# Reads of the turned exponentials and query loads from a second queue, early blocks turned in half steps 4, 5 and 12

## The chip, the cores and the metric

The kernel runs on one core of one Trainium2 chip. The metric is the device time of one execution in microseconds (us), as the median of repeated runs. Before the change it is 977.36 us (three runs, 975.66 to 977.53).

## What is computed

Packed attention followed by a Fourier mixing step and a feed-forward network, all in float32. `B` is 8, `S` is 576, there are 8 heads of 64 and 32 packed queries; `dm` is 512.

```
packed = softmax(p k^T / 8) v            # 32 rows for each head
x      = softmax(q packed^T / 8) packed  # 576 rows for each head
u      = x + real(fft(fft(x, axis=1), axis=2))
un     = (u - mean(u)) / sqrt(var(u) + 1e-6)
out    = u + relu(un @ w_ch1) @ w_ch2    # 512 -> 2048 -> 512
```

## The kernel before

The rows of all eight batches are cut into blocks of 128: four for each batch (`E0`, `O0`, `E1`, `O1`) and one `R` for each pair of batches, 36 in all. Four blocks make a tile of the feed-forward network, so there are nine tiles, t = 0 to 8. Tile 0 is batch 0. From tile 2 on a tile straddles batches: tile 6, for example, is E1 and O1 of batch 5, the R of batches 4 and 5, and E0 of batch 6.

`ffn` runs one tile. For each of 16 column chunks j it does `up(j)` (twelve matmuls into the single PSUM bank `ph`, L903), then `down(j - 1)` (twelve matmuls into four banks `acc`, L920). Every float32 product is three float32r products of a high and a low part. After `up(j)`, ScalarE makes `hh` (L909) and VectorE makes `hl` (L910); both read `ph`, so `up(j + 1)` may begin only when `hl` is done. The high and low parts of the weights (`wr_h` by ScalarE at L107, `wr_l` by GpSimd at L110) are made again for every tile, three pairs ahead.

Between the parts lie 32 half steps: `step(2j)` stands between `up(j)` and `down(j - 1)`, `step(2j + 1)` behind `down(j - 1)`. During tile t each half step advances the generator `front(t + 1)`, the attention and the transforms of the next batch, by one piece; half steps 1 and 2 finish the batch before it (its R block). The string `ORDER` lists the pieces, and each `y` is the end of one half step. For the batches from 2 on, which are made in tiles 1 to 6, half step 0 holds the scores and exponentials of two groups of four heads (`S`) and their way through memory (`D`); half step 3 holds `X`; 4 holds `p0 p1`, the matmuls of `packed` (`po`, L417); 5 the transposes `pptp` (`d0 d1`); 6 the first products `pg` (`g0`); 7 the score matmuls of the queries (`U`, tiles `s2T` and `s2Tt`); 12 to 15 `m0 a0 m1 a1`.

`D` is `scores_away`. The exponentials must stand with the keys on the partitions. VectorE transposes them in 32x32 pieces (`e1b`, L370), SyncE writes each group to memory (`fare`, L374, one DMA for each group), and four DMAs for each group read them back in turned order (`e1T`, L381). The first `po` matmuls read the `e1T` of group 0, the next ones that of group 1. All these DMAs, and the two query loads `qt` behind them, are on SyncE's queue in this order.

The blocks of the next tile, too, must be turned before the tile begins. `Turned.send(i)` does it for block i: VectorE subtracts the mean (`unp`, L827), transposes 32x32 pieces (`unt`, L830), SyncE writes them away (`far`, L832) and reads them back in four DMAs (`back`, L837). `sends(i)` calls `send_next` as often as half step i occurs in `SENDS`, and `send_next` takes the first block that isn't sent and whose mean is known; if there is none, nothing is sent. At the beginning of tile t those blocks of tile t + 1 are known that belong to earlier batches: one in tiles 1 and 2, two in tiles 3 and 4, three in tiles 5 and 6, all four in tile 7.

The order on TensorE, VectorE, ScalarE and GpSimd is the order in which the code is written. On SyncE a scheduler sets it, save for DMAs that are pinned with `keep_in_program_order`. `bd`, `unp`, `turned` and other tiles share one tag (`tmp`) of three buffers; `qt` and the keys `kp` share one (`ld`) of two; `e1`, `e1b`, `e1T` share one (`att`) of four.

Of the kernel before, what the change touches and what calls it, by code (L numbers as in the profile page):

```python
# [9 lines left out]
F32 = mybir.dt.float32  # L10
# [7 lines left out]
P = 128  # L18
S = 576
HS = S // 2  # L20
D = 64
NPK = 32
DM = 512
ATT = 4
# [17 lines left out]
         "H1 v2 W10 P1",  # L42
         "K0 K1 Q0 Q1 y S V0 V1 y X y p0 p1 y d0 d1 y g0 y U y g1 y e0 y e1 y y m0 y a0 y m1 y a1 y f0 y r0 y h0 y f1 y r1 y "
         "h1 y y",
         "V0 V1 S D Q0 Q1 y X y p0 p1 y d0 d1 y g0 y U y g1 y e0 y e1 y y m0 y a0 y m1 y a1 y f0 y r0 y h0 y f1 y r1 y "
         "h1 y y")


# [3 lines left out]
TOPS = [1, 1, 1, 1, 2, 1, 1, 2, 1, 1, 0, 1, 1, 1, 1, 1, 0, 1, 0, 1, 0, 1, 1, 0, 1, 1, 0, 0, 0, 0, 0, 0]  # L52
BITS = [2, 2, 1, 3, 1, 2, 1, 1, 1, 0, 1, 2, 1, 1, 0, 1, 0, 1, 0, 0, 0, 1, 2, 2, 0, 1, 1, 0, 0, 0, 0, 0]
SQUARES = [4, 7, 12, 16]
SENDS = (5, 12, 15, 27, 27)
NJ = 16
MANUAL = {getattr(mybir.EngineType, n) for n in ("PE", "DVE", "Activation", "Pool")}
NE = 288
# [25 lines left out]
def tile_kernel(ctx, tc, kpT, qT, v, w1, w2, tabH, tabL, tabR, tabF, tabB, tabT, sel, ident_d, out):  # L84
    nc = tc.nc
    B = kpT.shape[0]
# [4 lines left out]
    work = ctx.enter_context(tc.tile_pool(name="work", bufs=2))  # L91
# [59 lines left out]
    def spot(n, part, shape):  # L151

        t = (w1f, w2f, ubuf[:, 5:, :])[n].rearrange("p j n -> p (j n)")[:, int(part * DM):]
        size = shape[1] * shape[2]
        return t[:, 0:size].rearrange("p (a n) -> p a n", a=shape[1])
# [56 lines left out]
    def load_weights(i):  # L212

        for _ in range(BITS[i]):
            bits(*topped.pop(0))
            fetch_free()
        for _ in range(TOPS[i]):
            tops(*coming.pop(0))
# [10 lines left out]
    now = {}  # L229
# [10 lines left out]
    def next_step():  # L240
        steps[0] = (steps[0] or 0) + 1
        for item in [x for x in due if x[0] <= steps[0]]:
            due.remove(item)
            item[1]()
# [19 lines left out]
            after(1, squares)  # L264
            after(2, deviation)

    def load(src, shape, name, place=None, pinned=False):
        if isinstance(place, tuple):
            t = spot(*place, shape)
        elif place:  # L270
            t = work.tile(shape, F32, tag=place, name=name, bufs=2)
        else:
            t = ld.tile(shape, F32, tag="ld", name=name)
        sent = nc.sync.dma_start(t, src)
        if pinned:
            tc.keep_in_program_order(sent)
        return t
# [4 lines left out]
        nc.tensor.matmul(o, ll, rh, start=False, stop=last)  # L282

    def front(b):
        kps, vts, qts, e1s, e1T, rinv = {}, {}, {}, {}, {}, {}
        pp2s, ppT, pph, ppl, bdh, bdl = {}, {}, {}, {}, {}, {}
        s2s, zs, as_, fh, fl, xh, xl, oh, ol, gh, gl = {}, {}, {}, {}, {}, {}, {}, {}, {}, {}, {}
        eos, fs, sums = {}, {}, {}
# [11 lines left out]
        def load_keys(g):  # L300
            kps[g] = load(kpT[b, :, 2 * g:2 * g + 2, :], [P, 2, S + NPK], "kp")

        def load_values(g):
            if b < 2:
                vt = load(v[b, :, g], [P, 5, 4 * D], "vt", (g, 4) if b == 0 else None, b == 1)
                vts[g] = [vt[:, c] for c in range(5)]
                return
            vt = load(v[b, :, g, 0:4], [P, 4, 4 * D], "vt", "wst", True)
            vts[g] = [vt[:, c] for c in range(4)]
            vts[g].append(load(v[b, :, g, 4], [P, 4 * D], "vt4", ("xh", "oh")[g], True))  # L310

        def load_queries(g):
            qts[g] = load(qT[b, :, 2 * g:2 * g + 2, :], [P, 2, S], "qt", (g, 7) if b == 0 else (2, 0) if b == 1 and g == 0 else (2, 2 * S / DM) if b == 1 else None, b > 1)

        def side(g, h):

# [48 lines left out]
        def scores_away(*gs):  # L365

            blocks = {}
            for g in gs:
                blocks[g] = work.tile([P, S], F32, tag="att", name="e1b", bufs=ATT)
                nc.vector.transpose(blocks[g], e1s[g])  # L370
            fars = {}
            for g in gs:
                fars[g] = dr.tile([P, S], F32, tag="fare", name="fare")
                tc.keep_in_program_order(nc.sync.dma_start(fars[g], blocks[g]))  # L374
            for g in gs:
                e1T[g] = work.tile([P, 4, 5, NPK], F32, tag="att", name="e1T", bufs=ATT)
                wide = e1T[g].rearrange("k h c p -> k h (c p)")
                for r in range(4):
                    n = NPK * (5 if r < 3 else 3)
                    at = 5 * NPK * r  # L380
                    back = nc.sync.dma_start(wide[r * 32:(r + 1) * 32, :, 0:n],  # L381
                                             fars[g][:, at:at + n].rearrange("(h k) n -> k h n", h=4))
                    tc.keep_in_program_order(back)

        def turned_scores(*gs):
# [73 lines left out]
        def queries(*gs):  # L459

            for g in gs:
                if g not in qts:
                    load_queries(g)

            tails = [bank("s2Tt")] + ([psf.tile([P, 512], F32, tag="ph", name="s2Tt")] if len(gs) == 2 else [])
            s2T = narrow(gs, lambda g, h: ppT[g][side(g, h):side(g, h) + D, h * NPK:(h + 1) * NPK],
                         lambda g, h, w: qts[g][side(g, h):side(g, h) + D, h // 2, w], "s2T", dict(zip(gs, tails)))
            for g in gs:
                s2s[g] = work.tile([P, 18, 32], F32, tag="att", name="s2", bufs=ATT)
            for c, w in ((1, slice(16, 18)), (0, slice(0, 16))):  # L470
                for g in reversed(gs):
                    nc.vector.transpose(s2s[g][:, w, :].rearrange("p a k -> p (a k)"), s2T[g][c])  # L472
# [118 lines left out]
        def folded_parts(g):  # L591
# [10 lines left out]
            def low():  # L602
# [3 lines left out]
            in_place("H", g, low)  # L606

        parts = {"S": lambda _: scores(0, 1), "U": lambda _: queries(0, 1), "D": lambda _: scores_away(0, 1),
                 "s": scores, "t": turned_scores, "p": packed, "d": packed_parts, "q": queries, "e": less_one, "m": less_mean, "g": values_spectrum, "a": weights, "f": folded, "r": folded_rest,
                 "h": folded_parts,  # L610
                 "T": load_tables, "B": lambda _: load_turn(), "K": load_keys, "V": load_values,
                 "Q": load_queries, "I": lambda _: nc.sync.dma_start(ident, ident_d),
                 "W": lambda i: fetch(i // 2, i % 2), "w": lambda i: tops(i // 2, i % 2),
                 "v": lambda i: (bits(i // 2, i % 2), topped.remove((i // 2, i % 2))),
# [119 lines left out]
        for t, base in enumerate((0, FO) if b else ()):  # L734
# [15 lines left out]
            h = work.tile([P, DM], F32R, tag="tmp", name="yr_h", bufs=3)  # L750
# [120 lines left out]
    def wsplits():  # L871

        for t, _ in enumerate(tiles):
            for n, j in [(0, 0)] + [x for j in range(1, NJ) for x in ((0, j), (1, j - 1))] + [(1, NJ - 1)]:
# [4 lines left out]
                yield  # L879

    def ffn(first, turned, step, nxt, alone):
        keys = turned.keys
        n = len(keys)
# [46 lines left out]
        def sends(i):  # L930
            for _ in range(SENDS.count(i) if nxt is not None and first else 0):
                nxt.send_next()
# [45 lines left out]

    ready, splits = [], wsplits()
    gen0 = front(0)  # L980
    cur = Turned(tiles[0][1])

# [22 lines left out]
    with tc.manual_schedule(engines=MANUAL):  # L1005
        for at in gen0:
            if at == "means":
                less_blocks(0, 1)
                for i in (0, 1):
                    for move in cur.moves(i):  # L1010
                        move()
            elif at == "rest":
                break
        cur.parts(0)
        cur.parts(1)
        less_blocks(2, 3)
        next(splits)
        gens = {1: front(1)}
        next(gens[1])
    spare.clear()  # L1020
    rest = gen0
    for t, (first, tk) in enumerate(tiles):

        gen = gens.pop(t + 1, None) or (front(t + 1) if t + 1 < B else iter(()))
        ended = []

        def step(i):

            next_step()
            if i in ((1, 2) if t else (0, 2)):  # L1030
                next(rest, None)
            elif not ended and next(gen, None) == "rest":
                ended.append(gen)
            if t == 0:
                load_weights(i)
            assert i < 2 * NJ - 1 or t + 1 >= B or ended

        nxt = Turned(tiles[t + 1][1]) if t + 1 < len(tiles) else None

        with tc.manual_schedule(engines=MANUAL):  # L1040
            ffn(first, cur, step, nxt, t + 1 >= B)
        cur, rest = nxt, gen
# [114 lines left out]
```

## Time and profile before

| | |
|---|---|
| median of three runs | 977.36 us (975.66 to 977.53) |
| profiled execution | 979.0 us, of which the traced span is 977.2 us |
| granted TensorE clock | 0.993 on average |
| TensorE, VectorE, ScalarE, GpSimd busy | 950.1, 586.4, 453.0, 461.7 us |
| tiles 2 to 6 by the trace | 104 to 106 us each |

The trace is of one execution. A timeline row gives start and duration in us, engine (PE is TensorE, DVE VectorE, ACT ScalarE, POOL GpSimd, SPq SyncE's queue), line, operation, tiles written and read, and in brackets the idle time ahead of it with what ended it. Matmuls are pipelined: a 128x512 matmul is shown 0.39 us long, but the next one starts 0.227 us after it, so the last 0.16 us of a row are its tail.

### The profile page before, as it was taken

Reading aid. Unit: us, or ns where it says so; the run is one execution under the profiler, and the core shown is the slowest. Engines: PE = TensorE matmul, PEld = TensorE weight load, DVE = VectorE, ACT = ScalarE, POOL = GpSimd, SP = SyncE. Lnnn points to the kernel's source line nnn. Section 1 sums busy time; section 2 is a strip of 40 time slices with the busy share of each in tenths; the row PEclk is TensorE's granted clock in tenths of the full one; section 3 lists DMA queues with packets and bytes.
Section 4 is the critical chain, followed back from the end, with each engine's and each line's share of the span. In section 5 each row is a group of like instructions: output and inputs, shape, how many; then the busy total and the mean of one; then the engine's idle time right before and its main releaser. Section 6 shows DMA issues by size and latency. Waiting matters only on the chain.

```text
span 977.2 us, 15222 instructions
## 1 busy us (share of the span) xinstructions
PE 950.1 (97%) x5622; PEld 776.4 (79%) x5622; DVE 586.4 (60%) x1184; ACT 453.0 (46%) x930; POOL 461.7 (47%) x397
## 2 busy tenths in 40 slices
PE   7999999999999999999999999999999999999997
PEld 4777787788877887788778887878777888887886
DVE  5888966587567856594658566774569452223111
ACT  5677754445444445444534444444444443333231
POOL 3136534554455534653455445543464354544442
PEclk9999999999999999999999999999999999999999
DMA  9565312400152015200540035100601010101001
GB/s 356 213 223 189 104 65 77 142 29 1 47 192 73 1 43 166 103 22 2 165 146 22 1 101 163 70 22 23 195 22 44 11 55 22 44 23 44 1 1 43
DMA packets 47338, 79.70 MB, mean 82 GB/s; under 512 B 6928, under 2 KB 27280, under 8 KB 47264
## 3 DMA queue, kind: packets, MB, share of 16 engines
q1 hardware_dynamic: 46224, 77.42, 23.9%
q0 software_dynamic: 1040, 1.31, 0.4%
q8 instruction: 44, 0.72, 0.3%
q14 instruction: 30, 0.25, 0.1%
HBM read 58.92 MB, written 19.79 MB: 81 GB/s over the span
## 4 chain that ended last, share of the span: by engine, by line
PE 83%; DVE 9%; ACT 3%; DMA 2%; issue 1%; SPq 1%; POOL 0%; DVEq 0%; ACTq 0%
PE acc L920 35%; PE ph L903 35%; DVE hl L910 1%; DVE w2f L203 1%; PE px L282 1%; PE px L280 1%; PE px L281 1%; DMA wst<-w 1%; DMA e1T<-fare 1%; PE idle L723 1%; DMA ident<-ident_d 1%; PE py L280 1%; PE py L282 1%; PE py L281 1%; PE s2T L328 1%
## 5 line engine op out<-in xcount | busy, mean ns | idle before, releaser
L110 POOL TENSOR_TENSOR wr_l<-w2f,wr_h 128x512 fp32r<-128x512 f32 x144 | 188.8, 1311 | 296.3 <-ACT wr_h L107 296.0
L110 POOL TENSOR_TENSOR wr_l<-w1f,wr_h 128x512 fp32r<-128x512 f32 x144 | 198.7, 1380 | 187.7 <-ACT wr_h L107 163.0
L910 DVE SCALAR_TENSOR_TENSOR hl<-ph,hh 128x512 fp32r<-128x512 f32 x144 | 99.0, 687 | 293.4 <-ACT hh L909 292.2
L903 PE MATMUL ph<-uh,wr_h 128*128 128x512 f32 (+1 forms) x580 | 227.3, 394 | 6.5 <-DVE hl L910 3.9
L920 PE MATMUL acc<-wr_h,hh 128*128 128x512 f32 x576 | 226.0, 392 | 0.0
L903 PE MATMUL ph<-ul,wr_h 128*128 128x512 f32 (+1 forms) x580 | 224.6, 389 | 0.5 <-DVE ul L110 0.5
L903 PE MATMUL ph<-uh,wr_l 128*128 128x512 f32 (+1 forms) x580 | 224.9, 390 | 0.0
L920 PE MATMUL acc<-wr_h,hl 128*128 128x512 f32 x576 | 224.8, 390 | 0.0
L920 PE MATMUL acc<-wr_l,hh 128*128 128x512 f32 x576 | 224.8, 390 | 0.0
L909 ACT ACTIVATE hh<-ph 128x512 fp32r<-128x512 f32 x144 | 86.1, 598 | 244.6 <-PE ph L903 235.2
L107 ACT CAST wr_h<-w1f 128x512 fp32r<-128x512 f32 x144 | 89.3, 620 | 173.6 <-PE acc L920 86.3
L903 PEld LDWEIGHTS ph<-uh,wr_h 128*128 128x128 f32 x580 | 108.9, 189 | 36.5 <-DVE s L472 7.6
L903 PEld LDWEIGHTS ph<-uh,wr_l 128*128 128x128 f32 x580 | 108.9, 189 | 22.9
L920 PEld LDWEIGHTS acc<-wr_h,hl 128*128 128x128 f32 x576 | 108.1, 188 | 23.2
L903 PEld LDWEIGHTS ph<-ul,wr_h 128*128 128x128 f32 x580 | 108.6, 188 | 21.7 <-DVE ul L110 1.0
L920 PEld LDWEIGHTS acc<-wr_h,hh 128*128 128x128 f32 x576 | 108.1, 188 | 21.8
L920 PEld LDWEIGHTS acc<-wr_l,hh 128*128 128x128 f32 x576 | 108.2, 188 | 21.0
L107 ACT CAST wr_h<-w2f 128x512 fp32r<-128x512 f32 x144 | 88.3, 614 | 33.8 <-PE acc L920 26.6
L254 ACT ACTIVATE junk<-ubuf,stat 128x512 f32<-128x512 f32 x36 | 25.8, 718 | 4.5 <-DVE stat L249 4.5
L968 DVE SCALAR_TENSOR_TENSOR ubuf<-acc,stat,ubuf 128x512 f32<-128x512 f32 x36 | 24.6, 744 | 3.6 <-PE acc L920 3.5
L110 DVE TENSOR_TENSOR yl<-py,yh 128x258 fp32r<-128x258 f32 x32 | 13.1, 425 | 19.5 <-ACT yh L107 18.8
L827 DVE TENSOR_SCALAR unp<-ubuf,stat 128x512 f32<-128x512 f32 x26 | 24.2, 932 | 0.4
(230 smaller groups left out, 1220.7 us busy)
## 6 DMA issues: line engine op xcount, KB each, us to landing
kp<-kpT SPq DMA_DIRECT2D x16, 608.0 KB, 4.9
out<-ubuf SPq DMA_DIRECT2D x36, 256.0 KB, 4.0
qt<-qT SPq DMA_DIRECT2D x12, 576.0 KB, 4.4
far<-unt SPq DMA_DIRECT2D x26, 256.0 KB, 2.0
back<-far SPq DMA_DIRECT2D x104, 64.0 KB, 2.0
vt<-v SPq DMA_DIRECT2D x12, 512.0 KB, 3.9
w1f<-w SPq DMA_DIRECT2D x9, 512.0 KB, 6.2
w2f<-w SPq DMA_DIRECT2D x9, 512.0 KB, 5.7
```

The lines of the kernel that those rows point to most:

```text
L107: copied = nc.scalar.copy(hi, src)
L110: (lo_eng or nc.vector).tensor_tensor(lo, src, hi.bitcast(F32), ALU.subtract)
L254: nc.scalar.activation(junk, u, AF.Square, bias=st[:, 1:2], scale=-sign, accum_out=st[:, 2:3])
L280: nc.tensor.matmul(o, lh, rh, start=first, stop=False)
L281: nc.tensor.matmul(o, lh, rl, start=False, stop=False)
L282: nc.tensor.matmul(o, ll, rh, start=False, stop=last)
L827: nc.vector.tensor_scalar(un, u_of[key].rearrange("p (c q d) -> p q c d", c=4, q=4), stat_of[key][:, 1:2], None, ALU.subtract)
L903: nc.tensor.matmul(ph[:, t], l[:, c * P:(c + 1) * P], r[:, c, t], start=(k == 0), stop=(k == 11))
L909: nc.scalar.activation(hh[:, :T], ph[:, :T], AF.Relu)
L910: nc.vector.scalar_tensor_tensor(hl[:, :T], ph[:, :T], 0.0, hh[:, :T].bitcast(F32), ALU.max, ALU.subtract)
L920: nc.tensor.matmul(acc[i], l[:, w], r, start=(j == 0 and k == 0), stop=(j == NJ - 1 and k == 2))
L968: nc.vector.scalar_tensor_tensor(u, acc[i], stat_of[keys[i]][:, 2:3], u, ALU.mult, ALU.add)
```

## The change

The reads of group 1's exponentials leave `scores_away` and become a function `scores_back`, which half step 2 calls with ScalarE's queue; group 0's stay on SyncE in half step 0. The query loads go from half step 0 to half step 3 and to ScalarE's queue. `SENDS` becomes (4, 5, 12, 27, 27). This holds for tiles 1 to 6 (the batches from 2 on); `SENDS` acts in tiles 1 to 7.

```
-         "V0 V1 S D Q0 Q1 y X y p0 p1 y d0 d1 y g0 y U y g1 ...
+         "V0 V1 S D y X Q0 Q1 y p0 p1 y d0 d1 y g0 y U y g1 ...
...
-SENDS = (5, 12, 15, 27, 27)
+SENDS = (4, 5, 12, 27, 27)
...
-            qts[g] = load(qT[b, :, 2 * g:2 * g + 2, :], [P, 2, S], "qt", ..., b > 1)
+            qts[g] = load(qT[b, :, 2 * g:2 * g + 2, :], [P, 2, S], "qt", ...,
+                          queue=nc.scalar if b > 1 else nc.sync)
...
-            for g in gs:
-                e1T[g] = work.tile([P, 4, 5, NPK], F32, tag="att", name="e1T", bufs=ATT)
-                wide = e1T[g].rearrange("k h c p -> k h (c p)")
-                for r in range(4):
-                    n = NPK * (5 if r < 3 else 3)
-                    at = 5 * NPK * r
-                    back = nc.sync.dma_start(wide[r * 32:(r + 1) * 32, :, 0:n],
-                                             fars[g][:, at:at + n].rearrange("(h k) n -> k h n", h=4))
+            away.update(fars)
+            scores_back(0, nc.sync)
+            now["back"] = lambda: scores_back(1, nc.scalar)
+
+        def scores_back(g, queue):
+            e1T[g] = work.tile([P, 4, 5, NPK], F32, tag="att", name="e1T", bufs=ATT)
+            wide = e1T[g].rearrange("k h c p -> k h (c p)")
+            for r in range(4):
+                n = NPK * (5 if r < 3 else 3)
+                at = 5 * NPK * r
+                back = queue.dma_start(wide[r * 32:(r + 1) * 32, :, 0:n],
+                                       away[g][:, at:at + n].rearrange("(h k) n -> k h n", h=4))
+                if queue is nc.sync:
                     tc.keep_in_program_order(back)
...
             next_step()
+            if i == 2 and t + 1 < B and t:
+                now.pop("back")()
             if i in ((1, 2) if t else (0, 2)):
                 next(rest, None)
```

Three places of tile 5 show how the instructions move (the line numbers of the changed kernel are some seven higher). First ScalarE, from the `hh` of `up(1)`, ahead of half step 2, to the `hh` of `up(2)`, ahead of half step 4. Before:

```order
L909 ACTIVATE hh<-ph 128x512
L107 CAST wr_h<-w2f 128x512
L107 CAST wr_h<-w1f 128x512
L254 ACTIVATE junk,stat<-ubuf,stat 128x512
L909 ACTIVATE hh<-ph 128x512
```

and changed:

```order
L916 ACTIVATE hh<-ph 128x512
L107 CAST wr_h<-w2f 128x512
L387 DMA e1T<-fare 32x4x160 x3
L387 DMA e1T<-fare 32x4x96
L107 CAST wr_h<-w1f 128x512
L254 ACTIVATE junk,stat<-ubuf,stat 128x512
L274 DMA qt<-qT 128x1152 x2
L916 ACTIVATE hh<-ph 128x512
```

ScalarE now issues six DMAs between the two `hh`; the row `junk` is there in tiles 1, 3 and 5 only, where an R block is finished.

Then VectorE in half steps 4 and 5 and up to the `hl` of `up(3)`. Before:

```order
L422 TENSOR_SCALAR pp_6712<-po,ri 128x128
L448 COPY ppT<-pptp 128x128
L453 TENSOR_TENSOR ppl<-pptp,pph 128x128
L448 COPY ppT<-pptp 128x128
L453 TENSOR_TENSOR ppl<-pptp,pph 128x128
L827 TENSOR_SCALAR unp<-ubuf,stat 128x512
L830 STREAM_TRANSPOSE unt<-unp 128x512
L910 SCALAR_TENSOR_TENSOR hl<-ph,hh 128x512
```

and changed:

```order
L429 TENSOR_SCALAR pp_6712<-po,ri 128x128
L834 TENSOR_SCALAR unp<-ubuf,stat 128x512
L837 STREAM_TRANSPOSE unt<-unp 128x512
L455 COPY ppT<-pptp 128x128
L460 TENSOR_TENSOR ppl<-pptp,pph 128x128
L455 COPY ppT<-pptp 128x128
L460 TENSOR_TENSOR ppl<-pptp,pph 128x128
L834 TENSOR_SCALAR unp<-ubuf,stat 128x512
L837 STREAM_TRANSPOSE unt<-unp 128x512
L917 SCALAR_TENSOR_TENSOR hl<-ph,hh 128x512
```

One send stands a half step earlier, and a second one, which was in half step 12, now stands ahead of this `hl`. That is so in tiles 3 to 6; in tiles 1 and 2, with one early block, the pair ahead of `hl` is gone.

Last VectorE in half steps 14 and 15, between the `hl` of `up(7)` and that of `up(8)`. Before:

```order
L910 SCALAR_TENSOR_TENSOR hl<-ph,hh 128x512
L491 TENSOR_REDUCE z_7024<-s_6841 128x18
L492 TENSOR_SCALAR d_7025<-z_7024 128x18
L493 TENSOR_SCALAR z_7024<-z_7024 128x18
L494 RECIPROCAL z_7024<-z_7024 128x18
L495 TENSOR_TENSOR s_6841<-s_6841,d_7025 128x576
L532 TENSOR_TENSOR s_6841<-s_6841,z_7024 128x576
L534 STREAM_TRANSPOSE a<-s_6841 128x576
L827 TENSOR_SCALAR unp<-ubuf,stat 128x512
L830 STREAM_TRANSPOSE unt<-unp 128x512
L910 SCALAR_TENSOR_TENSOR hl<-ph,hh 128x512
```

and changed:

```order
L917 SCALAR_TENSOR_TENSOR hl<-ph,hh 128x512
L498 TENSOR_REDUCE z_7035<-s_6851 128x18
L499 TENSOR_SCALAR d_7036<-z_7035 128x18
L500 TENSOR_SCALAR z_7035<-z_7035 128x18
L501 RECIPROCAL z_7035<-z_7035 128x18
L502 TENSOR_TENSOR s_6851<-s_6851,d_7036 128x576
L539 TENSOR_TENSOR s_6851<-s_6851,z_7035 128x576
L541 STREAM_TRANSPOSE a<-s_6851 128x576
L917 SCALAR_TENSOR_TENSOR hl<-ph,hh 128x512
```

The send of half step 15 is gone from here; the one in half step 12 stays, with the third early block in place of the second.

More of the change, by code (lines that the diff above doesn't have):

```diff
@@ L44 @@
          "h1 y y",
-         "V0 V1 S D Q0 Q1 y X y p0 p1 y d0 d1 y g0 y U y g1 y e0 y e1 y y m0 y a0 y m1 y a1 y f0 y r0 y h0 y f1 y r1 y "
+         "V0 V1 S D y X Q0 Q1 y p0 p1 y d0 d1 y g0 y U y g1 y e0 y e1 y y m0 y a0 y m1 y a1 y f0 y r0 y h0 y f1 y r1 y "
          "h1 y y")
@@ L265, in statistics, with load @@
             after(2, deviation)
-    def load(src, shape, name, place=None, pinned=False):
+    def load(src, shape, name, place=None, pinned=False, queue=nc.sync):
         if isinstance(place, tuple):
@@ L273, in load @@
             t = ld.tile(shape, F32, tag="ld", name=name)
-        sent = nc.sync.dma_start(t, src)
+        sent = queue.dma_start(t, src)
         if pinned:
@@ L284, in front @@
     def front(b):
-        kps, vts, qts, e1s, e1T, rinv = {}, {}, {}, {}, {}, {}
+        kps, vts, qts, e1s, e1T, rinv, away = {}, {}, {}, {}, {}, {}, {}
         pp2s, ppT, pph, ppl, bdh, bdl = {}, {}, {}, {}, {}, {}
@@ L312, in load_queries @@
         def load_queries(g):
-            qts[g] = load(qT[b, :, 2 * g:2 * g + 2, :], [P, 2, S], "qt", (g, 7) if b == 0 else (2, 0) if b == 1 and g == 0 else (2, 2 * S / DM) if b == 1 else None, b > 1)
+            qts[g] = load(qT[b, :, 2 * g:2 * g + 2, :], [P, 2, S], "qt", (g, 7) if b == 0 else (2, 0) if b == 1 and g == 0 else (2, 2 * S / DM) if b == 1 else None,
+                          queue=nc.scalar if b > 1 else nc.sync)
         def side(g, h):
```

## Prediction

> **What bounds the kernel now.** I read the page first, for the engine that is never free.
>
> ```profile
> span 977.2 us, 15222 instructions
> PE 950.1 (97%) x5622; PEld 776.4 (79%) x5622; DVE 586.4 (60%) x1184; ACT 453.0 (46%) x930; POOL 461.7 (47%) x397
> ```
>
> TensorE is busy for 97% of the span. The change takes no matmul away, so only TensorE's idle time can be won. The next view is the list of its waits from 160 to 800 us, which is tiles 1 to 6, where the change acts:
>
> ```profile
> PE ph L903 <- DVE hl L910: 2.9, 2, 1.5
> PE po L417 <- DMA e1T<-fare: 1.5, 3, 0.8
> PE po L417 <- ACT wr_h L107: 1.1, 2, 0.6
> PE po L417 <- PE po L417: 0.5, 1, 0.5
> ```
>
> That is the whole list: two waits for `hl`, and six (3 + 2 + 1) ahead of `po`, one for each tile; the named releasers differ, but the place is the same. The busy table by tile (tiles 4, 5, 6, cut at like places) says where the two are:
>
> ```profile
> 476.40:580.40 104.00, 103.44 (x631) 84.83 (x630) 68.62 (x141) 47.12 (x101) 51.15 (x43) 1.00 0.25 79
> 580.50:686.20 105.70, 103.75 (x631) 84.77 (x630) 68.96 (x144) 48.27 (x103) 51.46 (x44) 1.00 0.24 77
> 686.30:792.30 106.00, 103.70 (x631) 84.74 (x630) 68.08 (x141) 47.31 (x101) 50.90 (x43) 1.00 0.21 65
> ```
>
> The same matmuls (x631, busy 103.4 to 103.8) take 104.0, 105.7 and 106.0 us: tiles 5 and 6, those with three early blocks, are some 1.7 to 2.0 us longer.
>
> **Term 1: the reads of group 1.** TensorE's timeline: the two groups of `po` in tile 0, where nothing is waited for, then in tiles 5 and 6.
>
> ```profile
> 68.61 1.32 PE L417 MATMUL po<-vt,e1T 128*32 128x64 f32 x80
> 596.62 0.77 PE L417 MATMUL po<-vt,e1T 128*32 128x64 f32 x40
> 597.87 0.77 PE L417 MATMUL po<-vt,e1T 128*32 128x64 f32 x40 [0.48 <-PE po L417]
> 704.03 0.77 PE L417 MATMUL po<-vt,e1T 128*32 128x64 f32 x40 [0.83 <-DMA e1T<-fare]
> ```
>
> Unhindered, group 1 follows group 0 after 1.32 - 0.77 = 0.55 us; in tile 5 it follows after 1.25. The loss is 0.70, the idle time of 0.48 and the 0.22 of tail that hides it. Six tiles lose 3.1 (the sum above) + 6 x 0.22 = 4.4 us. SyncE's queue in tile 5, and what the reads and writes take in all tiles:
>
> ```profile
> 590.07 1.29 SPq L374 DMA_DIRECT2D fare<-e1b  x2
> 592.22 3.91 SPq L381 DMA_DIRECT2D e1T<-fare  x8
> 596.23 0.84 SPq L274 DMA_DIRECT2D qt<-qT  x2
> L381 SPq DMA_DIRECT2D e1T<-fare x48: 303/430/439, 175.5 to 701.3; - x48
> DMA to landing us min/median/max: 1.9/2.0/2.5
> 592.20:596.20 4.00, 4.00 (x19) 3.31 (x18) 3.24 (x10) 1.44 (x3) 2.58 (x2) 1.00 0.60 154
> ```
>
> The eight reads go out one each 0.47 to 0.49 us (3.91 / 8; 0.43 of it the instruction). The last starts at 596.13 - 0.43 = 595.70 and lands 2.0 later, at 597.7: `po` starts at 597.87. Now the writes: the second one starts at 590.07 + 1.29 - 0.32 = 591.04, and as the first read waited until 592.22 for the write of 590.07, the second write has landed 2.1 to 2.2 later, at 593.2. ScalarE can then issue group 1's four reads while SyncE is at its third and fourth: last start 593.2 + 3 x 0.47 = 594.6, landed at 596.6 to 597.1. TensorE wants them at 596.62 + 0.55 = 597.17. So the wait ends in most tiles, by 0.1 to 0.6 us of room. The DMA engines are 0.60 busy in this stretch (last row, last but one column): the eight reads need some 0.6 x 3.9 = 2.3 us of them and get 2.4 from first issue to last, so they queue little. I take nine tenths of the term: **-4.0 us**, with bounds of 0 and -4.4.
>
> **Term 2: the send of half step 15.** TensorE in tiles 5 and 6, VectorE in tile 5, and the same place of tile 3, which has no send there:
>
> ```profile
> 638.38 0.50 PE L903 MATMUL ph<-uh,wr_h 128*128 128x512 f32 x1 [1.46 <-DVE hl L910]
> 744.55 0.50 PE L903 MATMUL ph<-uh,wr_h 128*128 128x512 f32 x1 [1.46 <-DVE hl L910]
> 635.05 0.78 DVE L534 STREAM_TRANSPOSE a<-s 128x576 f32<-128x576 f32 x1
> 635.75 1.25 DVE L827 TENSOR_SCALAR unp<-ubuf,stat 128x512 f32<-128x512 f32 x1
> 637.04 0.71 DVE L830 STREAM_TRANSPOSE unt<-unp 128x512 f32<-128x512 f32 x1
> 637.67 0.65 DVE L910 SCALAR_TENSOR_TENSOR hl<-ph,hh 128x512 fp32r<-128x512 f32 x1
> 427.50 0.65 DVE L910 SCALAR_TENSOR_TENSOR hl<-ph,hh 128x512 fp32r<-128x512 f32 x1
> 428.53 0.39 PE L903 MATMUL ph<-uh,wr_h 128*128 128x512 f32 x1
> ```
>
> `up(9)` waits for `hl`, and `hl` stands behind `unp` and `unt`. Each stall costs 1.46 and the tail of 0.16: 1.62, or 3.2 for both, which fits the longer tiles. Without the send `hl` starts at 635.8 and ends at 636.5, and `up(9)` can start at 638.38 - 1.62 = 636.76. Tile 3 is that case already: `hl` ends at 428.15, `up(9)` starts unhindered at 428.53. The send that takes this block is the one of half step 12, whose place is filled in tiles 3 to 6 now without a wait. **-3.2 us**, bounds -3.2 and, if VectorE's lateness comes back elsewhere, 0.
>
> **Term 3: two sends ahead of the `hl` of `up(3)`, tiles 3 to 6.** In tile 5:
>
> ```profile
> 601.74 0.29 DVE L448 COPY ppT<-pptp 128x128 f32<-128x128 f32 x1 [2.69 <-PE pptp L446]
> 603.41 1.61 POOL L110 TENSOR_TENSOR bdl<-bd,bdh 128x256 fp32r<-128x256 f32 x2
> 603.91 0.51 DVE L827 TENSOR_SCALAR unp<-ubuf,stat 128x512 f32<-128x512 f32 x1
> 605.32 0.69 DVE L910 SCALAR_TENSOR_TENSOR hl<-ph,hh 128x512 fp32r<-128x512 f32 x1
> 605.92 1.29 DVE L514 TENSOR_TENSOR turned<-pg,turn 128x516 f32<-128x516 f32 x2
> 608.17 0.38 DVE L472 STREAM_TRANSPOSE s<-s2Tt 128x64 f32<-128x64 f32 x2 [0.17 <-PE s2Tt L328]
> 607.86 1.06 PE L328 MATMUL s2T<-qt,ppT 64*32 64x512 f32 x16
> 608.86 0.50 PE L903 MATMUL ph<-uh,wr_h 128*128 128x512 f32 x1
> ```
>
> The send moved to half step 4 falls into VectorE's idle 2.69 us ahead of `ppT`: free. The second one is no longer third but fourth in the line of `tmp` tiles behind `bd`, `bd`, so it takes the first `bd`'s buffer and must wait until GpSimd has read it, at about 604.2 (half of the row of 1.61), by when the second `bdl` runs; `unp`, 0.51 here and 1.25 beside GpSimd above, then ends near 605.1 instead of 604.42. `hl` slips by 0.3 to 0.8, and `turned` with it: its second half, which empties a bank that `s2T` needs, ends at 607.5 to 608.0 against 607.86, and the `s2Tt` transposes that free `ph` end their first half at 608.4 to 608.9 against 608.86. So 0 to 0.3 us in each of four tiles; **+0.4 us**, bounds 0 and +2.4 (0.6 each). On SyncE the second `far` now stands ahead of the key loads and its `back` reads between them; nothing needs either before the tile's end. Tile 7 has no `front`, so its sends lie beside matmuls.
>
> **Term 4: what six issues do to ScalarE.** No ScalarE DMA is in this trace; SyncE's 0.47 us is the nearest row. ScalarE in tile 5:
>
> ```profile
> 591.49 0.61 ACT L107 CAST wr_h<-w2f 128x512 fp32r<-128x512 f32 x1
> 593.83 0.62 ACT L107 CAST wr_h<-w1f 128x512 fp32r<-128x512 f32 x1 [1.73 <-PE acc L920]
> 595.05 0.73 ACT L254 ACTIVATE junk<-ubuf,stat 128x512 f32<-128x512 f32 x1 [0.59 <-DVE stat L249]
> 596.78 0.60 ACT L909 ACTIVATE hh<-ph 128x512 fp32r<-128x512 f32 x1 [0.92 <-PE ph L903]
> ```
>
> It stands free from 592.10, waits for the write until 593.2, issues until 595.0 (idle time up to 593.83, so 1.2 us late), casts to 595.6, squares to 596.5, issues the two query loads to 597.4, and `hh` starts 0.6 late; in tiles 2, 4 and 6, without `junk`, on time. Behind it wait `wr_h`, whose pair is not used before `up(3)`, behind `pptp`, and `hl`, `pp` and `pptp` itself: VectorE was through with `pp` at 601.74 - 2.69 = 599.05 and `pptp` ended about 601.7, so there is some 2 us of room. The loads start at about 596.5, as before (596.23), and are needed by `s2T` at 607.86. Cost 0; if the room is gone, the price is the last rival's.
>
> **Sum.** -4.0 - 3.2 + 0.4 = -6.8. The span becomes 970.4 and the profiled execution 979.0 - 6.8 = 972.2; the median of the runs is 1.6 below that execution, so I say 977.4 - 6.8 = **970.6 us**. The best case by the bounds is -7.6, 969.8; I go 0.4 below it, since the three runs shown already lie 1.9 apart.
>
> **Rivals.**
> *One issuer's pace for both queues.* If two queues share what makes a DMA's issue take 0.47 us, the eight reads alternate and still take 8 x 0.47 = 3.8 us: `po` waits as before, and ScalarE is held until 595.9 instead of 595.0. Then `hh` comes 1.5 late, `bd` and `bdl` slip by 0.5 to 1, and `s2T` waits some 0.3 to 0.5 in four tiles: 0 - 3.2 + 1.4, or **975.6 us**. For it: a read's issue takes 0.30 at the least and 0.43 in the median, as if one that follows another at once waited for something of it. Against it: that something can as well be SyncE's own sequencer, and no row has two queues at once. The Trainium skill has the rule, in Perfetto Trace Analysis, section DMA Instruction — HWDGE (DVE, Sync): an issuing sequencer locks a descriptor generator that it shares, and the lock wait is part of the instruction's time; no run here shows it yet, and by it the sum would be that of this rival.
> *The double send bites.* Term 3 at its bound, or the stall of half step 15 back in 12: -4.0 - 3.2 + 2.4, some **972.6 us**. Against it: it takes `unp` at its slowest in all four tiles, and tile 3 carries a send in half step 12 without a wait.
> *ScalarE's issues are dear: slower.* The longest of SyncE's issues that I use as a bound:
>
> ```profile
> L274 SPq DMA_DIRECT2D vt<-v x26: 328/364/1016, 60.9 to 691.4; - x26
> ```
>
> At 1.0 us each, the reads end at 597.2 and land after 598.1 (`po` loses 0.25 more), `hh` comes near 600.7, and `pptp` waits about 1.3 to 2: +1.6 to +2.2 in six tiles less 3.2, about +8, **985 us**. It decides from some 0.75 us for an issue, where the 2 us of room are gone. Against it: the median of 0.36 to 0.43.
>
> **How the numbers follow.** The forecast has 0.62 (969.4 to 972.2), the shared pace 0.20, the double send 0.10, the dear issue 0.08. The range is 969.4 to 976.2: all but the last and some tails. 0.2% of 977.4, about what a measurement of this kernel tells from no change, is 2.0 us. Half of the shared pace lies above 975.4, so faster 0.62 + 0.10 + 0.10 = 0.82, same 0.10, slower 0.08.
>
> **What will show it.** TensorE's waits from 160 to 800 us: no `po` row if term 1 holds (two groups in one row of 1.32), `po` still at 3 us if the pace is shared; no `hl` row if term 2 holds; a wait of `s2T` or `ph` near half step 7 in tiles 3 to 6 sizes term 3. ScalarE's `e1T` issues at 0.43 us, with SyncE's unchanged beside them, refute the shared pace; over 0.6 us, in either queue, speak for it. A `pptp` wait means that ScalarE is too late. I am wrong if the tiles don't all come to some 103.5 us.

## The result, and the profile after

The changed kernel takes **970.58 us** (median of six runs, 969.59 to 972.46); the kernel before 976.84 us (six runs, 975.23 to 977.53). The ratio is 0.9943, with a 95% interval of 0.9932 to 0.9953: 6.3 us faster, against a forecast of 970.6. The profiled execution took 969.8 us. First the page of it: span, busy times and, from the list of DMA queues (packets, MB, share of the 16 engines' span), the one that is new.

```profile
span 968.0 us, 15186 instructions
PE 946.9 (98%) x5622; PEld 775.5 (80%) x5622; DVE 590.4 (61%) x1184; ACT 452.5 (47%) x930; POOL 463.8 (48%) x397
q10 hardware_dynamic: 5184, 8.85, 2.9%
```

The span is 9.2 us shorter. The matmuls are the same 5622. q10 is ScalarE's: group 1's reads and the query loads. TensorE's list of waits from 160 to 800 us, four rows before, is now one:

```profile
PE po L424 <- ACT wr_h L107: 1.1, 2, 0.6
```

So `po` still waits twice, in tiles 1 and 3. The list names ScalarE, but in both the last read of group 1 landed 0.36 and 0.24 us ahead of the end of the wait, which is what a wait for that read looks like: in tile 5 of `qt_early`, below, the step from landing to `po` is 0.20. The busy table of tiles 1 to 6, cut at the places that answer to those of before:

```profile
160.60:264.80 104.20, 103.65 (x634) 85.10 (x633) 69.80 (x143) 47.64 (x102) 51.69 (x43) 1.00 0.18 61
264.90:368.90 104.00, 103.94 (x636) 85.40 (x635) 69.54 (x140) 47.26 (x101) 51.73 (x43) 1.00 0.23 74
369.00:472.95 103.95, 103.35 (x631) 84.95 (x630) 71.04 (x144) 47.75 (x102) 51.70 (x44) 1.00 0.25 78
473.05:576.27 103.22, 103.22 (x631) 84.97 (x630) 70.47 (x141) 47.22 (x101) 51.41 (x43) 1.00 0.25 79
576.37:679.77 103.40, 103.40 (x631) 84.92 (x630) 69.76 (x144) 48.12 (x103) 51.73 (x44) 1.00 0.25 79
679.87:783.16 103.29, 103.29 (x631) 84.88 (x630) 68.93 (x141) 47.24 (x101) 51.20 (x43) 1.00 0.21 67
```

Tiles 4, 5 and 6 were 104.0, 105.7 and 106.0 long; now TensorE is busy through each (length and first busy time agree), and the two tiles with three early blocks are no longer than the others. Tiles 1 and 3 are not at 103.5: TensorE idles 0.55 and 0.60 us in them. (Tiles 1 and 2 have four matmuls more than the others.)

Not all of the 9.2 us is the change. The same table for the first 60 us, tile 0 but for its end, before and then after (the column to read is the third from the end, the granted clock):

```profile
0.00:60.00 60.00, 49.71 (x459) 38.63 (x460) 44.17 (x109) 35.93 (x73) 17.40 (x35) 0.91 0.68 245
```
```profile
0.00:60.00 60.00, 50.09 (x472) 38.83 (x473) 45.47 (x115) 38.35 (x83) 18.42 (x35) 0.97 0.72 260
```

Nothing is changed in tile 0, yet 472 matmuls fit into the 60 us where it was 459: in this execution TensorE's clock was halved for less of the time. I paired the matmul records of the two traces one by one and took how much later each starts: 3.35 us of the 9.2 lie in tile 0, and 5.85 us behind it. Those 5.85 are the two `hl` waits (3.47), `po` in tiles 1 to 6 (2.1) and small shifts.

### The profile page after: what moved, and what is told of

Read it like the earlier page. It is cut to its first block, busy times and chain, and to the rows that moved or that the text cites. A ratio compares the mean times of both kernels' runs of the same rounds, so it can differ in the third digit from the quotient of the medians.

```text
span 968.0 us, 15186 instructions
## 1 busy us (share of the span) xinstructions
PE 946.9 (98%) x5622; PEld 775.5 (80%) x5622; DVE 590.4 (61%) x1184; ACT 452.5 (47%) x930; POOL 463.8 (48%) x397
## 4 chain that ended last, share of the span: by engine, by line
PE 88%; DVE 5%; ACT 3%; DMA 2%; issue 1%; SPq 0%; POOL 0%; DVEq 0%; ACTq 0%
PE ph L910 38%; PE acc L927 38%; DMA w1f<-w 2%; PE px L282 1%; PE px L280 1%; PE px L281 1%; PE po L424 1%; PE py L280 1%; PE py L282 1%; PE py L281 1%; PE s L329 1%; DVE hl L917 1%; DVE w1f L203 1%; DVE w2f L203 1%; PE s2T L329 1%
## 5 line engine op out<-in xcount | busy, mean ns | idle before, releaser
L258 POOL TENSOR_TENSOR stat<-stat,mhalf 128x1 f32<-128x1 f32 x36 | 23.5, 664 | 2.8 <-DVE stat L257 2.8
```

Of the source, the lines that this page charges most:

```text
L258: nc.gpsimd.tensor_tensor(st[:, 2:3], st[:, 2:3], mhalf, ALU.pow)
```

## The experiments

Each expectation below was written ahead of its run. "At `po`" is the sum over tiles 1 to 6 of how much sooner TensorE gets through `po` than in the trace of before, matmul by matmul; a negative number means sooner. The kernel before was run beside each of two sets of experiments, on two chips: 976.68 us beside the first (`sends_only`, `queue_only`, `qt_later`, `qt_early`), 976.58 us beside the second.

### Half of the change: the sends alone

`sends_only` is the kernel before with one line of the change:

```
-SENDS = (5, 12, 15, 27, 27)
+SENDS = (4, 5, 12, 27, 27)
```

> The kernel before with SENDS = (4, 5, 12, 27, 27) alone; reads and query loads stay on SyncE. Theory (the parts add up): the two waits for hl in tiles 5 and 6 vanish, the six waits ahead of po stay at some 3 us in the list: 3.5 us faster than before (0.36%). Rival (the double send ahead of the hl of up(3) costs what the prediction allowed): a wait of ph or s2T near half step 7 in tiles 3 to 6, 0.1 to 0.6 us each, and only 1 to 3 us faster.

Measured: 972.16 us, ratio 0.9952 (0.9937 to 0.9967), 4.5 us faster than before. TensorE's waits:

```profile
PE po L417 <- DMA e1T<-fare: 1.8, 4, 0.5
PE po L417 <- ACT wr_h L107: 0.6, 1, 0.6
```

Both `hl` waits are gone (-3.47 us matmul by matmul), no `s2T` or `ph` wait takes their place in tiles 3 to 6, and `po` still waits in five tiles. At `po` the sum is -0.7 although nothing was changed there: that much it varies between executions.

### The other half: the queue alone

`queue_only` is the changed kernel with the old `SENDS`:

```
-SENDS = (4, 5, 12, 27, 27)
+SENDS = (5, 12, 15, 27, 27)
```

> The changed kernel with SENDS = (5, 12, 15, 27, 27) as before; group 1's reads and the query loads on ScalarE. Theory (the parts add up): po as in the changed kernel, the two hl waits stay at 2.9 us: 2.1 us faster than before (0.2%). Rival (the queue change helps or hurts through ScalarE's lateness, too): hl or pptp waits that the kernel before does not have, and less than 1 us or more than 3.5 us faster.

Measured: 975.89 us, ratio 0.9987 (0.9977 to 0.9996), 0.8 us faster than before. By time alone that is below the 1 us at which the rival was to hold, but the interval runs from 0.4 to 2.2 us, and the list has none of the new `hl` or `pptp` waits that the rival needs:

```profile
PE ph L910 <- DVE hl L917: 2.9, 2, 1.5
PE po L424 <- DMA e1T<-fare: 0.9, 1, 0.9
PE po L424 <- PE po L424: 0.3, 1, 0.3
```

The `hl` waits are back at their old 2.9 us. At `po` -1.9 us, half of what I forecast; in tile 3 the last read lands 3.58 us after its issue and `po` waits 0.9. So the smaller gain does not come from the sends: it is in the queues. In time the two halves, 4.5 and 0.8 us, add up to 5.3, about the whole.

### The query loads a half step later, and half steps sooner

In the changed kernel's trace the query loads stand where I had not put them. ScalarE in tile 5 (ACT its operations, ACTq the DMAs that its sequencer issues):

```profile
589.04 1.79 ACTq L387 DMA_DIRECT2D e1T<-fare  x4
590.92 0.62 ACT L107 CAST wr_h<-w1f 128x512 fp32r<-128x512 f32 x1 [2.96 <-DVE stat L249]
591.01 0.84 ACTq L274 DMA_DIRECT2D qt<-qT  x2
591.45 0.72 ACT L254 ACTIVATE junk<-ubuf,stat 128x512 f32<-128x512 f32 x1
592.59 0.60 ACT L916 ACTIVATE hh<-ph 128x512 fp32r<-128x512 f32 x1 [0.33 <-PE ph L910]
```

They are issued while the cast runs, 0.6 us behind the last read (issued at 590.38), ahead of the `junk` that is written ahead of them. Two kernels move them. `qt_later`, one half step later:

```
-         "V0 V1 S D y X Q0 Q1 y p0 p1 y ...
+         "V0 V1 S D y X y Q0 Q1 p0 p1 y ...
```

> The changed kernel with the two query loads one half step later, behind the hh of up(2), so that they start after group 1's reads have landed. Theory Q (the reads land late in the changed kernel because the query loads, issued 0.5 us behind them, take the DMA engines): reads land 2.0 to 2.3 us after issue, po waits in no tile, 1.5 to 2.0 us faster than the changed kernel, some 7.7 faster than before (0.79%). Theory R (the reads delay each other, as two queues issue them at twice the rate): landing 2.5 to 3.2 us and po as in the changed kernel, 5.8 us faster than before.

Measured: 971.00 us, ratio 0.9942 (0.9925 to 0.9958): 5.7 us faster than before, where 7.7 was expected, so the time does not tell it from the changed kernel. In the trace there is a difference: from 160 to 800 us TensorE's list of waits is empty, and at `po` it is -3.5 us. The first load now goes out 2.2 us after the last read (issued at 591.77):

```profile
594.00 0.85 ACTq L274 DMA_DIRECT2D qt<-qT  x2
```

The last of ScalarE's four reads lands 2.1 to 2.5 us after its issue, where it took 2.2 to 3.2 in the changed kernel (3.02, 2.77, 3.23, 2.20, 2.50, 2.26 in tiles 1 to 6).

`qt_early` puts the loads in half step 0, on SyncE behind group 0's reads:

```
-         "V0 V1 S D y X Q0 Q1 y p0 p1 y ...
+         "V0 V1 S D Q0 Q1 y X y p0 p1 y ...
...
-            qts[g] = load(qT[b, :, 2 * g:2 * g + 2, :], [P, 2, S], "qt", ...,
-                          queue=nc.scalar if b > 1 else nc.sync)
+            qts[g] = load(qT[b, :, 2 * g:2 * g + 2, :], [P, 2, S], "qt", ..., b > 1)
```

> The changed kernel with the query loads on SyncE in half step 0, behind group 0's reads, so that they start while ScalarE is still at group 1's. Theory Q: the last reads land 3 to 4 us after issue, po waits in all six tiles, 0.5 to 1.2 us each, and the kernel is 1.5 to 4 us slower than the changed one (2 to 4.5 faster than before). Theory R: po as in the changed kernel, 5.8 us faster than before.

Measured: 1004.51 us, ratio 1.028 (1.0257 to 1.0303), some 28 us slower than before; the direction was expected, the size not. TensorE's waits; SyncE and ScalarE in tile 5; TensorE there:

```profile
PE po L423 <- DMA e1T<-fare: 18.1, 5, 4.1
PE po L423 <- issue: 4.2, 1, 4.2
```
```profile
611.03 1.77 SPq L386 DMA_DIRECT2D e1T<-fare  x4
613.01 0.94 SPq L274 DMA_DIRECT2D qt<-qT  x2
611.98 1.76 ACTq L386 DMA_DIRECT2D e1T<-fare  x4
```
```profile
615.42 0.77 PE L423 MATMUL po<-vt,e1T 128*32 128x64 f32 x40
620.40 1.29 PE L423 MATMUL po<-vt,e1T 128*32 128x64 f32 x40 [4.21 <-issue]
622.64 0.63 PE L926 MATMUL acc<-wr_h,hl 128*128 128x512 f32 x1
623.07 0.63 PE L926 MATMUL acc<-wr_h,hh 128*128 128x512 f32 x1
```

ScalarE's last read is issued at 613.29, 0.28 us behind the first query load, and lands at 620.20; group 1's `po` starts at 620.40. In the six tiles the last read takes 5.9 to 6.9 us. And the matmuls behind the wait come 0.43 us apart, not 0.227. The granted clock says why (third column from the end):

```profile
622.00:623.00 1.00, 1.00 (x3) 0.79 (x3) 0.96 (x3) 0.00 (x0) 0.78 (x1) 0.50 0.06 16
626.00:627.00 1.00, 1.00 (x7) 0.80 (x6) 0.29 (x1) 0.88 (x3) 0.18 (x1) 1.00 0.28 84
```

Each such wait costs itself (2.7 to 3.8 us at `po` against before, 19.3 in all) and then 1.5 to 2.1 us of matmuls at half the clock, in all six tiles; the mean clock of this execution is 0.982. Another 1.6 us lie in tile 0, where the edit changes nothing: a stretch at half the clock from 82.4 us on, which no other trace has.

### Both queues back on one

`reads_sync` is `qt_later` with group 1's reads on SyncE, behind group 0's, so that only the second queue is taken away:

```
-            now["back"] = lambda: scores_back(1, nc.scalar)
+            scores_back(1, nc.sync)
...
-            if i == 2 and t + 1 < B and t:
-                now.pop("back")()
```

> As the one before, but group 1's reads go back to SyncE, behind group 0's in half step 0; ScalarE issues the query loads alone. Theory P (the second queue is what brings the reads forward): the last read is issued 3.3 us after the first instead of 2.3, lands 2.0 to 2.1 us later, and po loses some 0.4 to 0.7 us in each tile, 3 to 4 in all: 3.5 to 4.2 us faster than before. Theory Q alone (only the query loads behind the reads were in their way): no po wait, as fast as with the later loads and both queues.

Measured: 973.42 us, ratio 0.9965 (0.995 to 0.998). Waits, and the reads (ns at the least, median, most; landing in us):

```profile
PE po L424 <- DMA e1T<-fare: 1.7, 3, 1.0
PE po L424 <- PE po L424: 0.7, 3, 0.3
L387 SPq DMA_DIRECT2D e1T<-fare x48: 303/430/917, 174.3 to 698.1; - x48
DMA to landing us min/median/max: 1.8/2.0/2.5
```

The reads land sooner than on two queues (2.0 against 2.5 in the median), but the eight are issued one behind another, and `po` waits in all six tiles: at `po` -0.6, no more than `sends_only`, and 3.2 us faster than before, where 3.5 to 4.2 was expected. So the second queue is what the gain at `po` comes from: the late place of the loads without it does not bring it.

### The changed kernel and the later loads again

`changed_again` is the changed kernel without an edit, `qt_later_again` is `qt_later`, both run beside `reads_sync`.

> The changed kernel once more, beside the next three. po loses 1.5 to 3 us in its six tiles, no hl wait, 5 to 6.5 us faster than before (0.5 to 0.67%).

> The query loads one half step later, once more, with the changed kernel on the same chip. Theory Q: no po wait again, about 7.2 us faster than before (0.74%) and 1.4 faster than the changed kernel. Rival (the missing po waits were one execution's luck): po as in the changed kernel, and no difference from it.

Measured: 972.35 us, ratio 0.9953 (0.9935 to 0.997), and 970.07 us, ratio 0.993 (0.9911 to 0.9949). The intervals overlap; in the traces it is -2.5 us at `po` with one wait, and -3.3 with none.

```profile
PE po L424 <- DMA e1T<-fare: 0.8, 1, 0.8
```

In `changed_again` the first 60 us have the clock of 0.91 that the trace of before has, and its tile 0 is as long as there; behind tile 0 it is 6.3 us shorter. The kernels stand so; the fourth column is how long after group 0's first `po` matmul that of group 1 starts, least and most of tiles 1 to 6. `two_at_five`, the next experiment, has the changed kernel's reads and loads:

| kernel | reads of group 1 | query loads | group 1 behind group 0, us | at `po`, us |
|---|---|---|---|---|
| before | SyncE, one queue | SyncE, half step 0 | 1.00 to 1.60 | 0 |
| `sends_only` | SyncE, one queue | SyncE, half step 0 | 0.77 to 1.34 | -0.7 |
| `reads_sync` | SyncE, one queue | ScalarE, half step 4 | 0.99 to 1.74 | -0.6 |
| changed | ScalarE | ScalarE, half step 3 | 0.68 to 1.37 | -2.1 |
| `changed_again` | ScalarE | ScalarE, half step 3 | 0.68 to 1.61 | -2.5 |
| `queue_only` | ScalarE | ScalarE, half step 3 | 0.68 to 1.71 | -1.9 |
| `two_at_five` | ScalarE | ScalarE, half step 3 | 0.68 to 1.03 | -3.2 |
| `qt_later`; again | ScalarE | ScalarE, half step 4 | 0.68 to 0.71; 0.68 to 0.83 | -3.5; -3.3 |
| `qt_early` | ScalarE | SyncE, half step 0 | 4.0 to 5.0 | +19.3 |

With the loads in half step 3, group 1 is more than 1 us behind in 6 tiles of 24 (four executions), with the loads in half step 4 in none of 12. That the loads in half step 3 cost something is therefore likely, and `qt_early` shows that they can; but the best of the four executions, -3.2, all but reaches the worst with the later loads, -3.3, so how much they cost is not settled.

### Two sends in half step 5

The changed kernel's two sends ahead of the `hl` of `up(3)` cost nothing. `two_at_five` puts the first one beside the second, so that both lie behind `ppl`:

```
-SENDS = (4, 5, 12, 27, 27)
+SENDS = (5, 5, 12, 27, 27)
```

> The changed kernel with SENDS = (5, 5, 12, 27, 27): in tiles 3 to 6 both early sends stand behind the transposes of half step 5, ahead of the hl of up(3). Theory (the send in half step 4 is free since VectorE is idle there, and the room behind the one in half step 5 is some 0.3 us): hl comes 1.2 to 1.7 us later than in the changed kernel, s2T or ph waits 0.8 to 1.5 us in each of the four tiles, 3 to 6 us slower than the changed kernel. Rival (hl has more room than that): no wait, as fast as the changed kernel.

Measured: 976.62 us, ratio 1.0001 (0.9988 to 1.0014), 4.3 us over `changed_again`, which was run beside it. TensorE's waits; then, in tile 5, VectorE from the second pair on (the row of its transposes, 0.71 us, is left out), and TensorE:

```profile
PE ph L910 <- DVE s L479: 3.9, 4, 1.0
```
```profile
602.16 0.45 DVE L834 TENSOR_SCALAR unp<-ubuf,stat 128x512 f32<-128x512 f32 x1
603.28 0.65 DVE L917 SCALAR_TENSOR_TENSOR hl<-ph,hh 128x512 fp32r<-128x512 f32 x1
603.85 1.28 DVE L521 TENSOR_TENSOR turned<-pg,turn 128x516 f32<-128x516 f32 x2
605.17 1.87 DVE L527 TENSOR_TENSOR turned<-turned 128x258 f32<-128x258 f32 x2
606.96 0.37 DVE L479 STREAM_TRANSPOSE s<-s2Tt 128x64 f32<-128x64 f32 x2
607.25 0.50 PE L910 MATMUL ph<-uh,wr_h 128*128 128x512 f32 x1 [0.98 <-DVE s L479]
```

With 1.2 us more ahead of `hl`, `turned` ends at 605.1 while `s2T` stood ready from 604.78, and the transposes that free `ph` come last: TensorE waits 1.0, once in each of tiles 3 to 6. Paired by matmuls it is 1.33 us a tile, 5.3 in all: some 0.27 at `s2T` and 1.05 at `ph`. This was expected at 0.8 to 1.5 a tile.

## Why the prediction was right, and which term was off

**Term 2, the send of half step 15: right.** -3.2 forecast, -3.47 found, in the changed kernel and in `sends_only`. VectorE and TensorE in tile 5:

```profile
630.33 0.78 DVE L541 STREAM_TRANSPOSE a<-s 128x576 f32<-128x576 f32 x1
631.03 0.65 DVE L917 SCALAR_TENSOR_TENSOR hl<-ph,hh 128x512 fp32r<-128x512 f32 x1
632.07 0.39 PE L910 MATMUL ph<-uh,wr_h 128*128 128x512 f32 x1
```

`hl` follows the transpose with no pair between, ends at 631.68, and `up(9)` starts at 632.07 without a wait, as in tile 3 before.

**Term 3, two sends ahead of `hl`: 0, forecast +0.4.** In tile 5 of the changed kernel:

```profile
599.46 0.94 DVE L834 TENSOR_SCALAR unp<-ubuf,stat 128x512 f32<-128x512 f32 x1 [0.18 <-POOL bdl L110]
601.07 0.65 DVE L917 SCALAR_TENSOR_TENSOR hl<-ph,hh 128x512 fp32r<-128x512 f32 x1
601.65 1.28 DVE L521 TENSOR_TENSOR turned<-pg,turn 128x516 f32<-128x516 f32 x2
603.15 1.06 PE L329 MATMUL s2T<-qt,ppT 64*32 64x512 f32 x16
604.14 0.50 PE L910 MATMUL ph<-uh,wr_h 128*128 128x512 f32 x1
```

The mechanism is there as described: `unp` waits for the `bdl` that reads its buffer (0.18) and takes 0.94 beside GpSimd. But `turned` ends at 602.93, 0.2 us ahead of `s2T`, so it costs nothing. The room is small: `two_at_five` overdraws it.

**Term 1, the reads of group 1: the direction right, the size not.** -4.0 forecast, -2.1 and -2.5 found in the two executions of the changed kernel. Two steps of the working failed. The first is the ceiling of 4.4. It took 0.55 us, from tile 0, as what group 1 needs behind group 0. In tiles 1 to 6 the distance is never below 0.68, in any of the kernels; tile 5 of the changed kernel, where nothing is waited for, has the two groups in one row of 1.45 and not of 1.32:

```profile
592.48 1.45 PE L424 MATMUL po<-vt,e1T 128*32 128x64 f32 x80
```

The six distances of before add up to 7.6 us, so the term could bring 7.6 - 6 x 0.68 = 3.5 and no more, and `qt_later` brings it all (-3.5). Why tile 0 needs 0.13 less is open. The second step stands in term 4: "squares to 596.5, issues the two query loads to 597.4". It took ScalarE's issues to stand in line behind its operations, 1.5 us after the reads in odd tiles and 0.6 us in even ones. They don't: the loads go out during the cast, 0.1 to 0.2 us after the last read's issue has ended. So the estimate that the eight reads "queue little" left out two loads of 590 KB (128 x 1152 x 4 bytes) on the same DMA engines, and the last read lands up to 3.2 us after its issue, where the working allowed 2.0 to 2.5. `qt_later` takes the loads away from there, and the last read lands after 2.1 to 2.5 us. The loads alone are not enough for the delay: in the kernel before they go out 0.5 us behind the last read, on its queue, and it lands after 2.0 to 2.5 us all the same. There the reads go out at half the rate; that this is the difference is not shown. The Trainium skill says in DMA: Bandwidth & Descriptors, section Issuing engines are not separate DMA queues, that the two queues use the same 16 DMA engines, and its rules add that a second issuer saves issue time alone. The runs agree: 2.5 us a read on two queues, 2.0 on one, and still `po` is sooner with two.

**Term 4, ScalarE's six issues: the cost of 0 right, its working not.** I had `hh` 0.6 us late in odd tiles; it was on time, and waited 0.33 us for TensorE in tile 5. What ScalarE's sequencer waits for the write, as the semaphore rows of the reads' line have it (ns at the least, median, most):

```profile
L387 ACTq EVENT_SEMAPHORE  x6: 38/2559/2581, 170.4 to 689.9; - x6
```

In tile 5 that wait began 2.56 us ahead of 589.04, at 586.5, when the `hh` and the cast written ahead of it were still to run (586.86 and 587.35). The sequencer is ahead of the datapath. The operation behind the reads still waits for their issue, as I had it: the cast starts at 590.92, 1.2 us later than before (593.83, less the 4.1 us by which the trace is ahead at `hh`). But the loads then cost nothing, since they go out beside the cast.

**The rivals.** One issuer's pace for both queues is refuted. The reads of the changed kernel:

```profile
L387 SPq DMA_DIRECT2D e1T<-fare x24: 318/424/439, 172.1 to 692.9; - x24
L387 ACTq DMA_DIRECT2D e1T<-fare x24: 332/444/460, 173.0 to 693.9; - x24
```

Two at once take 0.424 and 0.444 us each in the median, where eight from SyncE alone took 0.430. The lock wait of the Trainium skill's Perfetto Trace Analysis, section DMA Instruction — HWDGE (DVE, Sync), which that rival rested on, shows no lengthening between these two queues here. The same rows refute the dear issue (it decides from 0.75 us). The double send costs time in `two_at_five` alone, where both sends lie in half step 5. The sign of being wrong that the prediction names last, tiles that don't all come to some 103.5, was there in part: tiles 1 and 3 don't, since `po` still waits in them.

**The total.** 970.6 forecast, 970.58 measured. The sum of -6.8 stands against 6.3 us between the medians, and against -5.85 and -6.3 in the traces behind tile 0. That the medians agree to 0.02 us is chance: term 1 was 1.5 to 1.9 too large, terms 2 and 3 together 0.7 too small, the forecast started from 977.36 where six runs of the kernel before gave 976.84, and the runs of one kernel lie up to 5.5 us apart (`reads_sync`).

Open stays why the four latest last reads with the loads right behind them (3.0 to 3.6 us, of 24) all lie in tiles 1 and 3, and whether the 2.3 us between `qt_later_again` and `changed_again` would hold over more runs.

## What to carry to other kernels

A second issuing queue can win back what the issues in line cost, as long as nothing large goes out just ahead of the small transfer that somebody waits for; its price has to be taken against the unhindered time of a place of the same kind, which tile 0 was not; place bulk loads by the time when their issue really happens, which on ScalarE is not behind the operations written ahead of them. A stall of an engine in order is often cured by moving one pair of instructions to a half step where that engine idles, but the room there has to be read from the trace: 1.2 us less of it was worth all of the 4.3 us gained. Before a difference of spans is explained, compare a stretch that was not changed: here a third of it lay there.

## What the runs showed of the hardware that I had not expected

- In `qt_early` the last read of each tile (32 x 4 x 96 x 4 bytes, 49 KB), issued 0.2 to 0.6 us behind the first of two loads of 590 KB on the other queue, landed after 5.9 to 6.9 us. The read ahead of it (82 KB), issued between 0.23 us ahead of that load and 0.06 us behind it, took 4.8 to 5.9. In `qt_later`, with the loads 2.2 us behind, the last read took 2.1 to 2.5.
- A wait of TensorE of 4.21 us was followed by matmuls at a granted clock of 0.50, 0.43 us apart. The Trainium skill has this in TensorE: Matmul & The Clock Gate, Part 1: an idle window of about 3.4 us halves the clock until the engine has been busy for as long again. The stretches agree: 3.4 us behind each of the six waits, 6.8 behind that of tile 5. The idle time need not be as long: in tile 5 TensorE stopped at 616.19 (615.42 + 0.77), and by the first row below, two us with a mean of 0.82, the clock was halved from 618.3, 2.1 us later. Waits of 3.25 to 4.21 us halved it in all six tiles; the waits of 1.46 us before the change did not. In between it is not settled: in the same execution a wait of 1.64 us that ended at 82.11 was followed by half the clock (second row), while the same wait, 1.62 to 1.65 us long in the nine other executions, was not.

```profile
617.00:619.00 2.00, 0.00 (x0) 0.00 (x0) 0.17 (x1) 0.00 (x0) 2.00 (x3) 0.82 0.62 244
82.37:85.78 3.41, 3.41 (x9) 2.66 (x9) 1.97 (x3) 0.67 (x2) 1.42 (x2) 0.50 0.65 173
```

- ScalarE's sequencer issues DMAs while its datapath is at work: two issues of 0.42 us began within the 0.62 us of one cast (tile 5 of the changed kernel).
